# Feed-forward products of batch 0 in float32 in place of three split passes, in a fused attention and two-MoE kernel

## The chip, the cores and the metric

The kernel runs on one core of a Trainium2 chip. The metric is the device time of one execution in microseconds; the span of the profiled execution runs from its first to its last instruction. The engines are PE (TensorE), PEld (its weight loads), ACT (ScalarE), DVE (VectorE), POOL (GpSimd) and SP (SyncE), whose queue issues the DMAs.

## The reference

Attention with a tanh cap on the scores over 4 batches of 12 heads (448 positions, 64 wide), then two feed-forward layers on the 1792 rows:

```python
scores = cap * np.tanh(scale * np.matmul(q, k.transpose(0, 1, 3, 2)) / cap)
attn = np.exp(scores - np.max(scores, axis=-1, keepdims=True))
attn = attn / (np.sum(attn, axis=-1, keepdims=True) + 1e-09)
x = np.matmul(attn, v)                      # as 1792 x 768
h = x @ w_in;  x = (h - np.tanh(h)) @ w_out                     # layer 0
h = x @ w_in2; out = (h / (1.0 + np.exp(-1.702 * h))) @ w_out2  # layer 1
```

Activations are float32. The weights (768 x 2048 and 2048 x 768, twice) arrive as float64.

## The kernel before

The attention of batch 0 runs alone. Then four batches of feed-forward work follow, `moe(b)` for b = 0 to 3, and beside batch b the attention of batch b+1: the program text issues a piece of attention after so many products, by `ATT_RATES` (for batch 0 none in the first quarter, then 0.7, 0.7 and 1.3 parts). Tensor products and attention share PE, which works through one queue in order.

`moe(b)` has four quarters of equal products: `gemm_in(0)`, `gemm_out(0)`, `gemm_in(1)`, `gemm_out(1)`. Each quarter has 96 products of a 128 x 128 weight tile with a 128 x 448 activation tile. The weights are cut into 68 chunks: a `gemm_in` has 16 chunks of 6 tiles, a `gemm_out` has 6 x 3 chunks of 6, 5 and 5 tiles (`parts`). A product is made in one of two ways. **Split**: weight and activation are each cut into a high part (float32r) and a low part, and three passes wh*xh, wh*xl and wl*xh (float32r) add up in PSUM. **Unsplit**: one float32 matmul on the uncut operands, which stands in the trace as two matmul records. Before the change only the 16 chunks of batch 0's first quarter are unsplit (`i < KF` in `w_split`); they read `xf`, and the split ones read `xh`, `xl` (or `gh`, `gl` behind the activation function).

In batch 0 each chunk is also converted from float64 (`w_convert`): `dbl_dma` loads its words into one of three `wd` buffers (pool `wd_p`); ACT scales the high words into a `wr` buffer (L193) and makes a 16-bit step on the low half-words in place (L194); DVE shifts (L195) and joins (L196); SP then issues the load of the chunk three further on into the freed `wd` buffer, and the store of the float32 result to DRAM (`kept`), from which batches 1 to 3 reload it. `wr_p` has three buffers. A split chunk is then cut: the high part on ACT or DVE (`hi_act`, `hi_dve`, L93 and L96), the low part on POOL in batch 0 (`lo_pool`, L102) and on DVE later (`lo_dve`, L99).

`ahead(i)`, called behind the first matmul of chunk i, converts up to chunk i + 2. The activation function of layer 0 is `g_cubic` (ACT L520, L528, L530, L531; DVE L521, L532, L534, L535), that of layer 1 `g_gate` (ACT L550, DVE L552); behind either, `g_split` cuts the result into `gh` (ACT or DVE in turn) and `gl` (POOL). `run_late` issues their last steps some matmuls into the next chunk. The output of layer 0 is cut into `xh`, `xl` by ACT and DVE. A scheduler sets the final order on each engine; it may pull an instruction up as far as its buffers allow.

Attention lines that the steps touch: transposes of q and k on PE (L275, tile `ps_qk`), scores (L290, L298, `ps_sc`), tanh (L306) and exp (L317) on ACT with the row maximum on DVE between (L307, L308), transposes of the weights (L359, `ps_pt`), products with v (L372, `ps_pv`), and a copy `xs` on ACT at the end of each pair of heads (L385).

## Time and profile before

| what | value |
|---|---|
| three runs, median (lowest to highest) | 1348.9 us (1344.34 to 1349.25) |
| the profiled execution, own time | 1349.95 us |
| its span | 1348.2 us |
| mean granted PE clock, share of full speed | 0.978 |
| PE / PEld busy | 1273.5 us (94%) / 1027.5 us (76%) |
| ACT / DVE / POOL busy | 845.6 us (63%) / 840.0 us (62%) / 329.0 us (24%) |
| DMA | 203.5 MB, mean 151 GB/s |

A busy share is an average over stages with different limits. Matmuls are pipelined, so a record of PE spans more than the time that it adds; the distance from one start to the next is what a matmul costs. "Idle before" with a releaser names what an engine waited for last.

### The profile page before, as it was taken

What the parts mean: (1) busy time and instruction counts of PE and PEld (TensorE: products, weight loads), DVE (VectorE), ACT (ScalarE), POOL (GpSimd) and SP (SyncE); (2) the same over time, 40 slices, a digit from 0 to 9 for tenths busy, and PEclk for the clock granted to TensorE, in tenths of its full rate; (3) what the DMA queues carried; (4) which work ended last, traced back from release to release, by engine and by line L of the source; (5) the groups of instructions that cost most, each with busy time, mean ns of one, the idle gap of its engine ahead of it and who ended that gap; (6) DMA issues with size and microseconds to landing.
All of it is one profiled execution on the core that took longest, in us unless ns stands there. A gap on an engine that the chain in (4) does not pass through costs nothing.

```text
span 1348.2 us, 18627 instructions
## 1 busy us (share of the span) xinstructions
PE 1273.5 (94%) x6540; PEld 1027.5 (76%) x6540; DVE 840.0 (62%) x1280; ACT 845.6 (63%) x1352; POOL 329.0 (24%) x258
## 2 busy tenths in 40 slices
PE   8989978888788998999999999999999999999998
PEld 3445557676666787888888888888898889999997
DVE  5867997567765569945657439845575528734432
ACT  7858979778778668745656437745565527623421
POOL 0002354346533214301232004301232103201300
PEclk8989998999999899999999999999999999999999
DMA  7305767866566386533334466433433257433332
GB/s 203 103 15 182 241 227 237 276 203 216 187 192 201 114 266 222 172 110 104 110 102 127 112 189 179 127 97 105 120 98 106 86 163 216 131 108 110 108 117 59
DMA packets 163981, 203.53 MB, mean 151 GB/s; under 512 B 53296, under 2 KB 120880, under 8 KB 163888
## 3 DMA queue, kind: packets, MB, share of 16 engines
q1 hardware_dynamic: 163888, 202.35, 49.5%
q8 instruction: 51, 0.84, 0.3%
q14 instruction: 42, 0.34, 0.1%
HBM read 156.99 MB, written 45.32 MB: 150 GB/s over the span
## 4 chain that ended last, share of the span: by engine, by line
PE 62%; ACT 9%; DVE 8%; issue 4%; POOL 2%; DMA 1%; SPq 0%; DVEq 0%; ACTq 0%; POOLq 0%
PE ps_y L588 30%; PE ps_h L568 21%; PE ps_pv L372 4%; PE ps_pt L359 3%; ACT wd L194 3%; PE ps_sc L290 3%; POOL wl L102 2%; ACT wr L193 1%; DVE wr L196 1%; ACT t L317 1%; DVE tm L307 1%; DVE g_q L534 1%; DVE g_q L535 1%; DVE g_t L532 1%; PE ps_o L613 1%
## 5 line engine op out<-in xcount | busy, mean ns | idle before, releaser
L99 DVE TENSOR_TENSOR wl<-wr,wh 128x768 fp32r<-128x768 f32 (+1 forms) x172 | 156.9, 912 | 217.9 <-PE ps_y L588 100.2
L588 PE MATMUL ps_y<-gh,wh 128*128 128x448 f32 x768 | 288.3, 375 | 4.1 <-DVE wh L96 3.4
L588 PE MATMUL ps_y<-gl,wh 128*128 128x448 f32 x768 | 291.2, 379 | 1.0 <-POOL gl L102 1.0
L568 PE MATMUL ps_h<-xh,wh 128*128 128x448 f32 x672 | 250.6, 373 | 19.1 <-DVE g_g L552 11.4
L93 ACT CAST wh<-wr 128x768 fp32r<-128x768 f32 (+1 forms) x189 | 148.4, 785 | 183.7 <-PE ps_y L588 136.6
L568 PE MATMUL ps_h<-xl,wh 128*128 128x448 f32 x672 | 249.3, 371 | 1.1 <-DVE xl L99 1.1
L588 PE MATMUL ps_y<-gh,wl 128*128 128x448 f32 x768 | 190.5, 373 | 0.0
L317 ACT ACTIVATE t<-t,tm,cpos 112x448 f32<-112x448 f32 x192 | 144.4, 754 | 41.5 <-DVE tm L308 37.6
L588 PEld LDWEIGHTS ps_y<-gh,wh 128*128 128x128 f32 x768 | 147.3, 192 | 22.9 <-issue 5.9
L588 PEld LDWEIGHTS ps_y<-gl,wh 128*128 128x128 f32 x768 | 147.4, 192 | 19.2 <-issue 6.8
L568 PE MATMUL ps_h<-xh,wl 128*128 128x448 f32 x672 | 161.3, 371 | 0.0
L588 PEld LDWEIGHTS ps_y<-gh,wl 128*128 128x128 f32 x768 | 143.1, 190 | 21.3 <-issue 9.9
L568 PEld LDWEIGHTS ps_h<-xh,wh 128*128 128x128 f32 x672 | 127.6, 190 | 37.5 <-DVE g_g L552 14.7
L102 POOL TENSOR_TENSOR gl<-g_q,gh 128x448 fp32r<-128x448 f32 x64 | 87.5, 1368 | 271.5 <-ACT gh L93 178.3
L568 PEld LDWEIGHTS ps_h<-xl,wh 128*128 128x128 f32 x672 | 127.4, 190 | 13.6 <-issue 2.1
L568 PEld LDWEIGHTS ps_h<-xh,wl 128*128 128x128 f32 x672 | 125.5, 189 | 14.9 <-issue 4.8
L102 POOL TENSOR_TENSOR gl<-g_g,gh 128x448 fp32r<-128x448 f32 x64 | 77.6, 1213 | 225.6 <-ACT gh L93 129.6
L307 DVE TENSOR_REDUCE tm<-t 112x2 f32<-112x896 f32 x96 | 103.4, 1080 | 45.7 <-ACT t L306 45.5
L102 POOL TENSOR_TENSOR wl<-wr,wh 128x768 fp32r<-128x768 f32 (+1 forms) x52 | 97.0, 1866 | 133.0 <-DVE wh L96 37.2
L194 ACT ACTIVATE wd<-wd 128x768 uint16<-128x768 uint16 (+1 forms) x68 | 125.9, 1852 | 1.0
L359 PE MATMUL ps_pt<-ident,t 112*112 112x112 f32 x768 | 97.2, 270 | 20.2 <-ACT t L306 13.1
L359 PEld LDWEIGHTS ps_pt<-ident,t 112*112 112x112 f32 x768 | 83.3, 139 | 42.3 <-ACT t L306 18.7
(76 smaller groups left out, 1698.4 us busy)
## 6 DMA issues: line engine op xcount, KB each, us to landing
wr<-kept SPq DMA_DIRECT2D x100, 384.0 KB, 3.0
wd<-in_moe_w_in_dram SPq DMA_DIRECT2D x64, 384.0 KB, 4.6
wr<-kept SPq DMA_DIRECT2D x72, 320.0 KB, 2.9
wd<-in_moe_w_out_dram SPq DMA_DIRECT2D x48, 384.0 KB, 4.2
kept<-wr SPq DMA_DIRECT2D x44, 384.0 KB, 5.1
wh<-kept_hl SPq DMA_DIRECT2D x32, 384.0 KB, 3.3
wl<-kept_hl SPq DMA_DIRECT2D x32, 384.0 KB, 3.7
kept<-wr SPq DMA_DIRECT2D x24, 320.0 KB, 4.7
```

What stands on the lines that cost most here:

```text
L93: nc.scalar.copy(out=dst, in_=src)
L99: nc.vector.tensor_tensor(out=dst, in0=src, in1=hi.bitcast(F32), op=ALU.subtract)
L102: nc.gpsimd.tensor_tensor(out=dst, in0=src, in1=hi.bitcast(F32), op=ALU.subtract)
L193: nc.scalar.mul(out=o, in_=high.bitcast(F32), mul=2.0 ** -112)
L194: nc.scalar.mul(out=half[:, :, :, 2], in_=half[:, :, :, 1], mul=F64_LOW)
L290: nc.tensor.matmul(ps[:, j, :S], qq[a, 0, c * CP:(c + 1) * CP], kk[a, 1], start=(m == 0), stop=(m == 2),)
L307: nc.vector.tensor_reduce(out=tm, in_=t, axis=AX.X, op=ALU.max)
L317: nc.scalar.activation(out=t[:, j], in_=t[:, j], func=AF.Exp, scale=cpos[:CP], bias=tm[:, j:j + 1], accum_out=ss[:, j, c:c + 1],)
L359: nc.tensor.transpose(ps[:, kc // 2, o:o + CP], t[:, j, kc * CP:(kc + 1) * CP], ident[:CP, :CP])
L372: nc.tensor.matmul(r_t[g][j * D:(j + 1) * D, :S], rawv[g][:, j, kc, :], p_t[g][:, kc, j, :], start=(kc == 0), stop=(kc == C - 1),)
L568: nc.tensor.matmul(ps[:, :S], w[:, kk, :], x[kk], start=(m == 0), stop=(m == len(seq) - 1))
L588: nc.tensor.matmul(ps[:, :S], w[:, f - f0, :], x[f], start=(c == 0 and m == 0), stop=(c == len(parts) - 1 and m == len(seq) - 1),)
```

## The change

Every product of batch 0 is made unsplit: `w_split` now takes all chunks with i < NCH as they are. The results of the activation function go to float32 tiles `gf`, which share the tags of `gh` (so `gh` is allocated when batch 1 begins), `g_split` does nothing in batch 0, and the output of layer 0 goes uncut to `xf`, by ACT and DVE in turn; `xh` is allocated when batch 1 cuts its input. `passes = 3` in `gemm_out` keeps the count of steps, and with it the pace of attention per chunk. Converted chunks are held in `wr_p` (even) and in the buffers of `wh_p` (odd), six in all, and `ahead` asks for four chunks ahead in place of two. For odd chunks the 16-bit step moves from ACT to DVE. PSUM tiles of odd f in batch 0's second `gemm_in` come from `ps_s`.

```diff
--- before.py
+++ after.py
@@ -35,6 +35,8 @@
 AHEAD = 2
 
 LATE_AT = 8
+
+LEAD_0 = 4
 
 WARM_UP = 12
 
@@ -148,7 +150,7 @@
     ]
     kept = [dr_p.tile([P, k1 - k0, P], F32, name=f"kept{i}") for i, (_, k0, k1) in enumerate(chunks)]
     dbls, raws, whl = {}, {}, {}
-    gh, gl = [], []
+    gf, gh, gl = [None] * KF, [None] * KF, []
     n_dma, n_split, n_use = [0], [0], [0]
 
     n_dbl = [0]
@@ -185,13 +187,21 @@
 
     def w_convert(i):
         _, k0, k1 = chunks[i]
-        r = wr_p.tile([P, WCH, P], F32, tag="wr", name="wr")
+        if i % 2:
+            r = wh_p.tile([P, WCH, P], F32, tag="wh", name="wr")
+        else:
+            r = wr_p.tile([P, WCH, P], F32, tag="wr", name="wr")
         d = dbls.pop(i)
         high, half = d[:, :, :, 1], d.bitcast(U16)
         o = r[:, :k1 - k0]
         u = o.bitcast(U32)
         nc.scalar.mul(out=o, in_=high.bitcast(F32), mul=2.0 ** -112)
-        nc.scalar.mul(out=half[:, :, :, 2], in_=half[:, :, :, 1], mul=F64_LOW)
+        if i % 2:
+            nc.vector.tensor_scalar(
+                out=half[:, :, :, 2], in0=half[:, :, :, 1], scalar1=F64_LOW, scalar2=None, op0=ALU.mult
+            )
+        else:
+            nc.scalar.mul(out=half[:, :, :, 2], in_=half[:, :, :, 1], mul=F64_LOW)
         nc.vector.tensor_scalar(out=u, in0=u, scalar1=3, scalar2=None, op0=ALU.logical_shift_left)
         nc.vector.scalar_tensor_tensor(
             out=u, in0=high, scalar=0x80000007, in1=u, op0=ALU.bitwise_and, op1=ALU.bitwise_or
@@ -209,14 +219,14 @@
             _, k0, k1 = chunks[i % NCH]
             n = k1 - k0
             r = w_convert(i) if i < NCH else raws.pop(i)
-            if i < KF:
+            if i < NCH:
                 whl[i] = (r, None)
                 n_split[0] += 1
                 continue
             h = wh_p.tile([P, WCH, P], F32R, tag="wh", name="wh")
             l = wh_p.tile([P, WCH, P], F32R, tag="wl", name="wl")
-            (hi_dve if i < NCH and i % 3 else hi_act)(h[:, :n], r[:, :n])
-            (lo_pool if i < NCH else lo_dve)(l[:, :n], r[:, :n], h[:, :n])
+            hi_act(h[:, :n], r[:, :n])
+            lo_dve(l[:, :n], r[:, :n], h[:, :n])
             if i // NCH == 1 and split_kept[i % NCH]:
                 for m, t in enumerate((h, l)):
                     nc.sync.dma_start(out=kept_hl[i % NCH][:, m], in_=t[:, :n].bitcast(F32))
@@ -399,6 +409,8 @@
         else:
             x = xs_p.tile([P, S], F32, tag="xs", name="xs")
             nc.sync.dma_start(out=x, in_=xd[i])
+        if xh[i] is None:
+            xh[i] = big.tile([P, S], F32R, tag=f"xh{i}", name=f"xh{i}")
         hi_act(xh[i], x)
         lo_dve(xl[i], x, xh[i])
 
@@ -508,11 +520,17 @@
 
     def ahead(i):
         w_dma(i + 2)
-        w_split(i + 2)
+        w_split(i + (LEAD_0 if i + LEAD_0 < NCH else 2))
 
     def g_split(f, g):
+        if gh[f] is None:
+            return
         yield (hi_dve if f % 2 else hi_act)(gh[f], g)
         yield lo_pool(gl[f], g, gh[f])
+
+    def g_tile(to, f, dt):
+        to[f] = g_big.tile([P, S], dt, tag=f"gh{f}", name=f"g{f}")
+        return to[f]
 
     def g_cubic(f, ps):
         t = g_p.tile([P, S], F32, tag="t", name="g_t")
@@ -531,7 +549,11 @@
             nc.scalar.activation(out=m, in_=v, func=AF.Relu, bias=cub_u)
             nc.vector.tensor_tensor(out=t, in0=v, in1=t, op=ALU.mult)
             next(last, None)
-            nc.vector.scalar_tensor_tensor(out=q, in0=q, scalar=CUB_C, in1=t, op0=ALU.add, op1=ALU.mult)
+            if gh[f] is None:
+                q_in, q = q, g_tile(gf, f, F32)
+            else:
+                q_in = q
+            nc.vector.scalar_tensor_tensor(out=q, in0=q_in, scalar=CUB_C, in1=t, op0=ALU.add, op1=ALU.mult)
             nc.vector.copy_predicated(out=q, mask=m.bitcast(U16), data=far)
             splits.append(g_split(f, q))
             for _ in last:
@@ -548,14 +570,14 @@
     def g_gate(f, ps):
         t = g_p.tile([P, S], F32, tag="t", name="g_t")
         nc.scalar.activation(out=t, in_=ps[:, :S], func=AF.Tanh, scale=0.5 * GELU_C)
-        g = g_p.tile([P, S], F32, tag="far", name="g_g")
+        g = g_tile(gf, f, F32) if gh[f] is None else g_p.tile([P, S], F32, tag="far", name="g_g")
         nc.vector.scalar_tensor_tensor(out=g, in0=t, scalar=1.0, in1=ps[:, :S], op0=ALU.add, op1=ALU.mult)
         late.append(lambda: list(g_split(f, g)))
 
     def gemm_in(layer, b):
         for f in range(KF):
             i, (wh, wl) = w_next()
-            if f % 4 == 3 if b > 0 else layer == 0 and f % 2:
+            if f % 4 == 3 if b > 0 else b == 0 and f % 2:
                 ps = ps_s.tile([P, 512], F32, tag="s", name="ps_h")
             else:
                 ps = ps_m.tile([P, 512], F32, tag="m", name="ps_h")
@@ -584,6 +606,10 @@
                 i, (wh, wl) = w_next()
                 seq = [p for f in range(f0, f1) for p in ((wh, gh, f), (wh, gl, f))]
                 seq += [(wl, gh, f) for f in range(f0, f1)]
+                passes = 1
+                if wl is None:
+                    seq = [(wh, gf, f) for f in range(f0, f1)]
+                    passes = 3
                 for m, (w, x, f) in enumerate(seq):
                     nc.tensor.matmul(
                         ps[:, :S], w[:, f - f0, :], x[f],
@@ -592,13 +618,13 @@
                     )
                     if m == 0:
                         ahead(i)
-                    if m == LATE_AT:
+                    if m == LATE_AT // passes:
                         run_late()
-                    if not (c == len(parts) - 1 and m == len(seq) - 1):
+                    for _ in range(passes - (c == len(parts) - 1 and m == len(seq) - 1)):
                         yield
-            if layer == 0:
-                if b == 0:
-                    xh[e] = big.tile([P, S], F32R, tag=f"xh{e}", name=f"xh{e}")
+            if layer == 0 and b == 0:
+                (hi_dve if e % 2 else hi_act)(xf[e], ps[:, :S])
+            elif layer == 0:
                 hi_act(xh[e], ps[:, :S])
                 lo_dve(xl[e], ps[:, :S], xh[e])
             else:
@@ -659,10 +685,12 @@
     first.close()
     g_big = pool("g_big", 1)
     ps_m = pool("ps_m", 2, space=bass.MemoryType.PSUM)
-    gh += [g_big.tile([P, S], F32R, name=f"gh{i}") for i in range(KF)]
     gl += [g_big.tile([P, S], F32R, name=f"gl{i}") for i in range(KF)]
     per_batch = 10 * NP
     for b in range(B):
+        if b == 1:
+            for f in range(KF):
+                g_tile(gh, f, F32R)
         n_pair[0] = n_split_x[0] = 0
         x_free[0] = False
         owed, live, cnt = 0.0, b + 1 < B, 0
```

Three places in the instruction order show what moves; line numbers of the changed kernel differ from those above (a few lines later).

ScalarE, while the attention of batch 0 runs, behind the second pair's exponentials. `wr<-wd` and `wd<-wd` are the two ScalarE steps of a conversion, `t,ss<-t` an exp, `t<-ps_sc` a tanh, `xs<-ps_pv` the end of a pair. Before:

```order
L194 ACTIVATE wd<-wd 128x768
L306 ACTIVATE t<-ps_sc,tsc 112x896
L317 ACTIVATE t,ss<-t,tm,cpos 112x448 x2
L193 ACTIVATE wr<-wd 128x768
L317 ACTIVATE t,ss<-t,tm,cpos 112x448
L385 COPY xs<-ps_pv 128x448
```

and with the change:

```order
L204 ACTIVATE wd<-wd 128x768
L198 ACTIVATE wr<-wd 128x768
L395 COPY xs<-ps_pv 128x448
L327 ACTIVATE t,ss<-t,tm,cpos 112x448 x2
L316 ACTIVATE t<-ps_sc,tsc 112x896
L198 ACTIVATE wr<-wd 128x768
L316 ACTIVATE t<-ps_sc,tsc 112x896
L327 ACTIVATE t,ss<-t,tm,cpos 112x448 x2
L316 ACTIVATE t<-ps_sc,tsc 112x896
L204 ACTIVATE wd<-wd 128x768
```

Before, three chunks (0 to 2) are converted ahead of the first product, the third around this place; now six are (0 to 5), chunks 3 and 4 here and chunk 5 four rows later. The rest of attention's ScalarE work stands behind them.

TensorE, the first chunk of `gemm_out(0)` in batch 0 (its last two of twelve high passes, its six low passes, and the first pass of the next chunk). Before:

```order
L588 MATMUL ps_y<-gh_1030,wh 128x448
L588 MATMUL ps_y<-gl_1046,wh 128x448
L588 MATMUL ps_y<-gh_1025,wl 128x448
L588 MATMUL ps_y<-gh_1026,wl 128x448
L588 MATMUL ps_y<-gh_1027,wl 128x448
L588 MATMUL ps_y<-gh_1028,wl 128x448
L588 MATMUL ps_y<-gh_1029,wl 128x448
L588 MATMUL ps_y<-gh_1030,wl 128x448
L588 MATMUL ps_y<-gh_1031,wh 128x448
```

and with the change the whole of that chunk and the first product of the next:

```order
L614 MATMUL ps_y<-g_1117,wr 128x448
L614 MATMUL ps_y<-g_1147,wr 128x448
L614 MATMUL ps_y<-g_1177,wr 128x448
L614 MATMUL ps_y<-g_1207,wr 128x448
L614 MATMUL ps_y<-g_1237,wr 128x448
L614 MATMUL ps_y<-g_1267,wr 128x448
L614 MATMUL ps_y<-g_1297,wr 128x448
```

Eighteen instructions of the chunk became six; nothing of a high or low part is waited for.

VectorE, one chunk of `gemm_in(0)` in batch 0, from one `g_far` to the next. Before:

```order
L521 TENSOR_TENSOR g_far<-ps_h,g_t 128x448
L96 CAST gh_1026<-g_q 128x448
L195 TENSOR_SCALAR wr<-wr 128x768
L532 TENSOR_TENSOR g_t<-g_v,g_t 128x448
L196 SCALAR_TENSOR_TENSOR wr<-wd,wr 128x768
L534 SCALAR_TENSOR_TENSOR g_q<-g_q,g_t 128x448
L535 COPY_PREDICATED g_q<-g_m,g_far 128x448
```

and with the change, at an odd chunk:

```order
L539 TENSOR_TENSOR g_far<-ps_h,g_t 128x448
L200 TENSOR_SCALAR wd<-wd 128x768
L205 TENSOR_SCALAR wr<-wr 128x768
L550 TENSOR_TENSOR g_t<-g_v,g_t 128x448
L206 SCALAR_TENSOR_TENSOR wr<-wd,wr 128x768
L556 SCALAR_TENSOR_TENSOR g_1267<-g_q,g_t 128x448
L557 COPY_PREDICATED g_1267<-g_m,g_far 128x448
```

The cast to `gh` is gone from every second chunk and the 16-bit step (L200) is new in every second chunk.

## Rows read from the trace of the kernel before

**Rows 1.** Windows by stage: us, PE, PEld, DVE, ACT, POOL busy (instructions), PEclk, DMA share, GB/s

```profile
100.30:172.60 72.30, 72.30 (x194) 36.27 (x192) 64.14 (x90) 67.79 (x95) 19.82 (x13) 1.00 0.67 212
172.60:482.40 309.80, 264.14 (x1382) 213.74 (x1381) 208.67 (x283) 239.06 (x321) 129.31 (x83) 0.94 0.66 208
...
796.10:1103.40 307.30, 303.57 (x1649) 256.43 (x1649) 185.24 (x308) 177.92 (x314) 67.08 (x56) 0.99 0.42 121
1103.40:1342.10 238.70, 238.70 (x1177) 218.36 (x1175) 116.75 (x160) 101.50 (x160) 39.38 (x32) 1.00 0.43 128
```

**Rows 2.** Chain that ended last, 90 to 470 us, its shares by line

```profile
by line: PE ps_y L588 12.7%; ACT wd L194 10.5%; issue 8.6%; POOL wl L102 7.3%; ACT wr L193 5.3%; DVE wr L196 4.8%; ACT t L317 3.9%; PE ps_pv L372 3.1%; DMA kept<-wr 2.4%; PE ps_sc L290 1.9%; DVE tm L307 1.9%; PE ps_pt L359 1.6%; ACT pf L93 
```

**Rows 3.** What PE waited for, 100 to 460 us: total us, times, longest

```profile
PE ps_pt L359 <- ACT t L306: 12.8, 5, 4.6
PE ps_h L568 <- DVE g_g L552: 11.4, 9, 3.0
PE ps_sc L290 <- ACT qk L93: 7.1, 4, 3.5
PE ps_sc L290 <- DVE ql L99: 4.1, 5, 1.2
```

**Rows 4.** PE timeline, first product of each batch and the last: start us, us, instruction

```profile
100.29 3.19 PE L568 MATMUL ps_h<-xf,wr 128*128 128x448 f32 x8
...
482.37 0.45 PE L568 MATMUL ps_h<-xh,wh 128*128 128x448 f32 x1
...
796.14 0.36 PE L568 MATMUL ps_h<-xh,wh 128*128 128x448 f32 x1
...
1103.41 0.36 PE L568 MATMUL ps_h<-xh,wh 128*128 128x448 f32 x1
...
1340.93 1.19 PE L588 MATMUL ps_y<-gh,wl 128*128 128x448 f32 x5
```

**Rows 5.** Lines by form, 100 to 460 us: busy us, mean ns | idle before

```profile
L194 ACT ACTIVATE wd<-wd 128x768 uint16<-128x768 uint16 x41 | 80.3, 1958 | 0.5
L568 PE MATMUL ps_h<-xf,wr 128*128 128x448 f32 x192 | 72.3, 539 | 0.0
...
L196 DVE SCALAR_TENSOR_TENSOR wr<-wd,wr 128x768 uint32<-128x768 uint32 x41 | 46.2, 1126 | 33.6 <-ACT wd L194 30.3 <-DMA raw<-in_q_dram 1.4 <-DMA kept<-wr 1.4
...
L193 ACT ACTIVATE wr<-wd 128x768 f32<-128x768 f32 x41 | 38.1, 929 | 28.1 <-POOL wl L102 24.1 <-DMA kept<-wr 3.9
...
L195 DVE TENSOR_SCALAR wr<-wr 128x768 uint32<-128x768 uint32 x41 | 26.5, 648 | 19.9 <-ACT wr L193 17.9 <-DMA wd<-in_moe_w_in_dram 1.9
```

**Rows 6.** ACT timeline, one ScalarE step of g_cubic, two chunks apart

```profile
142.89 0.62 ACT L520 ACTIVATE g_t<-ps_h 128x448 f32<-128x448 f32 x1
...
152.35 0.61 ACT L520 ACTIVATE g_t<-ps_h 128x448 f32<-128x448 f32 x1
```

**Rows 7.** DVE timeline, one chunk of the first quarter and the step before

```profile
158.11 0.61 DVE L534 SCALAR_TENSOR_TENSOR g_q<-g_q,g_t 128x448 f32<-128x448 f32 x1
...
159.39 0.60 DVE L521 TENSOR_TENSOR g_far<-ps_h,g_t 128x448 f32<-128x448 f32 x1
...
161.80 1.55 DVE L534 SCALAR_TENSOR_TENSOR g_q<-g_q,g_t 128x448 f32<-128x448 f32 x1
...
164.01 0.63 DVE L521 TENSOR_TENSOR g_far<-ps_h,g_t 128x448 f32<-128x448 f32 x1
```

**Rows 8.** ACT timeline, ends of the first three pairs of batch 0's attention

```profile
33.28 0.51 ACT L385 COPY xs<-ps_pv 128x448 f32<-128x448 f32 x1
...
47.57 0.53 ACT L385 COPY xs<-ps_pv 128x448 f32<-128x448 f32 x1 [0.17 <-PE ps_pv L372]
...
60.31 0.51 ACT L385 COPY xs<-ps_pv 128x448 f32<-128x448 f32 x1
```

**Rows 9.** What PE waited for in batch 1, 482 to 796 us

```profile
PE ps_h L568 <- DVE g_far L521: 5.7, 2, 5.0
```

## The prediction, made before the result was known

> **What bounds the kernel now.** I read the windows by stage first. Batches 2 and 3 keep PE busy for 303.6 of 307.3 us and for all of 238.7 us, at a granted clock of 0.99 and 1.00; the first quarter of batch 0 is just as full. The rest of batch 0 is not: 264.1 us busy in 309.8 us at a clock of 0.94 [rows 1]. The change touches batch 0, and only its last three quarters can give time back. The first products of the batches, at 100.29, 482.37, 796.14 and 1103.41 us, bound the stages [rows 4]; batch 0 takes 382.1 us, batch 1 313.8 us.
>
> Next, what ends last there. In the chain of waits from 90 to 470 us, much stands on the making of weights: the two conversion steps on ACT (10.5% and 5.3%), the low part on POOL (7.3%), the join on DVE (4.8%) [rows 2]. The lines say why: the first conversion step sat idle 28.1 us before it, 24.1 us of that until POOL had made a low part, which frees the `wr` buffer [rows 5]. So conversion runs three buffers round a loop that POOL closes, and it has little lead. The waits of PE itself show the other half: 12.8 us in which attention's transposes wait for a tanh on ACT, 7.1 and 4.1 us for the high and low parts of q and k, and 11.4 us until the gate on DVE frees a PSUM tile [rows 3]. The engines named there also do conversions, in order.
>
> **Part 1: more PE work.** The first quarter, unsplit and without attention, has 96 products in 192 records and takes 72.3 us [rows 5]. Batch 3, split and without attention, takes 238.7 us for four quarters [rows 1], 59.7 us each with the transposes of the output in it. A quarter made unsplit so costs PE 12.6 us more, three of them 37.8 us. This lies wholly on PE's path. [...]
>
> **Part 2: time that PE loses.** Attention beside a batch costs PE what batch 2 takes over batch 3: 307.3 - 238.7 = 68.6 us [rows 1]. Batch 0, as it is, would without lost time take 72.3 + 3 x 59.7 + 68.6 = 320.0 us; it takes 382.1, so 62.1 us are lost to waits and to the lower clock that goes with them. With the change the floor is 4 x 72.3 + 68.6 = 357.8 us. What of the 62.1 us stays?
>
> The buffer loop goes: POOL makes no low part in batch 0, there are six buffers in place of three, and PE itself frees them. ACT now takes 9.46 us for two chunks of the first quarter [rows 6], 4.73 us each, against 72.3 / 16 = 4.52 us on PE: it falls behind. Half of the 16-bit steps (1958 ns each [rows 5]) leave it, so 0.98 us per chunk, and it needs 3.75 us. DVE takes 4.62 us for a chunk in which one operation took 1.55 us where its fellow before took 0.61 us [rows 7]; without that stretch 3.68 us. The 16-bit step on DVE is not in this trace. Its bounds are the shift, 648 ns on as many words in rows without gaps, and ACT's own step on the same half-words, 1958 ns; I take 1126 ns, the join, which reads words at the same distance on the same engine [rows 5]. Half of it per chunk gives 4.25 us, with the upper bound 4.66 us: just under the pace of PE or just over it, and five converted chunks (22.6 us of PE work) cover 16 x 0.14 us. In the later quarters, where attention is added to PE's pace, or no cubic function runs, there is more room.
>
> [...]
>
> What does not go are waits within attention: PE in order behind tanh, exp, q and k. Batch 1, which has no conversions, loses 313.8 - 307.3 = 6.5 us against batch 2, 5.7 us of it in one line of waits [rows 4, 9]. I take 12 us for batch 0, about twice that, since ACT and DVE still convert beside attention; the bounds are 2 us (as batch 2) and 30.5 us (the three attention waits of [rows 3], 24.0 us, in full, and batch 1's 6.5). Batch 0 then takes 369.8 us, 12.3 us less than now.
>
> **Part 3: attention of batch 0 is made longer.** The order shows six chunks converted before the first product, where three are now. The load of chunk 3 waits for the end of conversion 0, and so on, and the loads of q, k and v queue behind those on SP; they were issued well ahead of their use, and I cost that at nothing. If that cover is gone, PE waits for q and k of a late pair. The conversions themselves delay attention on ACT and DVE: the pair with a conversion in it takes 47.57 - 33.28 = 14.29 us, the next, without, 12.74 us [rows 8]: 1.55 us for one, 4.7 us for three. The bounds are nothing and 14.0 us (three times the four steps of [rows 5], 4.66 us, with none of it hidden); a gain is excluded, since work is only added. In the first quarter PE is full already, so the early conversions are not paid back there.
>
> **Part 4: the rest.** Casts to high parts on ACT and DVE, low parts of activations on POOL, and the subtraction behind layer 0 all go; I cost them at nothing beyond part 2, since what they held up is counted in the 62.1 us. The stores to `kept`, the reloads and batches 1 to 3 stay; so does the work at the batch's end, where `gh` takes over buffers whose readers are done.
>
> **The sum**: -12.3 + 4.7 = -7.6 us. The profiled execution took 1349.95 us (span 1348.2), 1.05 us above the median of the three runs, 1348.9 us. So 1342.3 us by the profile and **1341.3 us** against the median.
>
> **The rivals.**
>
> *Nothing is lost any more (faster).* For it: with a longer time per chunk, ACT and DVE have longer to deliver attention's parts, and batch 2 loses hardly anything. Against it: ACT and DVE carry 17 conversions in each quarter. Lost 2 us, attention 2 us longer: 359.8 + 2 - 382.1 = -20.3 us, 1328.6 us.
>
> *The saving is eaten evenly (no change).* PE's extra 37.8 us and part 3 just equal what is won where 19.6 us stay lost: 1348.9 us. For it: batch 0's PE waits are as much attention's as the conversions' [rows 3].
>
> *Attention's waits stay (slower).* Place: PE's queue, at the transposes and scores of batch 1's attention in the last three quarters. In order behind conversions that themselves wait (for a load, or until PE frees a buffer), ACT delivers tanh and the parts of q and k as late as now. Lost 30.5 us, with 4.7 us for part 3: 357.8 + 30.5 + 4.7 - 382.1 = +10.9 us, 1359.8 us. It decides once more than 19.6 us stay lost. Against it: POOL no longer closes the loop.
>
> *The change doesn't do what it says.* If conversion still had no lead, say because three `wd` buffers and the loads bind, we would see lost time near the 62.1 us and far more than any of these; but the first quarter already converts a chunk in 4.73 us with these three buffers, and batch 0 needs one per 369.8 / 68 = 5.4 us. I give it 2%, inside the slower case.
>
> **How the numbers follow.** The forecast (5 to 17 us lost) gets 0.47, nothing lost 0.20, no change 0.16, slower 0.17. A measurement of this kernel can tell about 0.5% from no change, 6.7 us; my likeliest time is hardly beyond it. Of the forecast's own range the part below 12.9 us lost (attention included as above) counts as faster, about six tenths: faster 0.20 + 0.29 = 0.49, same 0.18 + 0.16 = 0.34, slower 0.17. The likeliest case alone spans 1334 to 1346 us. The range of 8 in 10 reaches into both outer cases, to 1327 us and 1357 us.
>
> **What the profile will show.** Right: first product of batch 0 at about 105 us, of batch 1 at about 475 us; the remaining batches as long as now; unsplit records near 72.3 / 192 = 0.377 us apart in all four quarters; PE's clock in 172 to 475 us above 0.97; no wait on POOL in the chain there; DVE's 16-bit step between 0.65 and 1.96 us; ACT's first conversion step no longer waiting for POOL. Wrong: PE waits on tanh or on q and k that add up to over 20 us, attention of batch 0 that ends at 110 us or later, or a quarter that takes over 100 us without such waits, which would mean that weights still come late.

## The result: faster, by more than twice what was forecast

The changed kernel takes 1329.08 us (median of 4 runs, 1326.04 to 1329.35), the kernel before, in 4 runs beside it, 1347.99 us: a ratio of 0.9856, 95% interval 0.984 to 0.9871. That is 18.9 us less, where 7.6 us less had been forecast. It lies inside the range, close to its lower end, and at the rival "nothing is lost any more" (1328.6 us).

The profiled execution took 1328.83 us, its span is 1327.0 us, 21.2 us below that of before. Batch 0 gives 26.6 us of it, the attention ahead of it takes 7.3 us back, and batches 1 to 3 give 1.9 us; batches 2 and 3 vary by as much between the traces of the kernels below (305.8 to 307.6 and 243.6 to 244.8 us). Windows of batch 0 by quarter, after (columns as in [rows 1]):

```profile
107.60:179.70 72.10, 72.10 (x194) 36.48 (x193) 59.51 (x97) 56.65 (x84) 0.00 (x0) 1.00 0.70 220
179.70:267.90 88.20, 88.20 (x317) 46.25 (x316) 51.09 (x80) 56.55 (x81) 1.28 (x4) 1.00 0.77 241
267.90:356.10 88.20, 88.20 (x322) 46.77 (x321) 55.43 (x83) 56.66 (x82) 1.08 (x3) 1.00 0.73 226
356.10:463.10 107.00, 107.00 (x459) 57.56 (x457) 55.29 (x85) 60.83 (x96) 2.95 (x6) 1.00 0.58 182
```

And quarters 2 and 3 of the kernel before:

```profile
173.10:273.50 100.40, 82.43 (x412) 67.73 (x413) 74.56 (x98) 81.09 (x101) 44.67 (x25) 0.93 0.78 248
273.50:370.80 97.30, 81.16 (x417) 66.09 (x417) 69.33 (x89) 78.90 (x107) 51.97 (x35) 0.96 0.63 200
```

PE is now busy for the whole of every quarter, at a clock of 1.00; before it stood idle for 16 to 18 us in each of these two, at 0.93 and 0.96. ACT's work in quarter 2 falls from 81.09 to 56.55 us, POOL's from 44.67 to 1.28. The first products of batches 0 and 1, in the PE timeline after:

```profile
107.58 1.31 PE L590 MATMUL ps_h<-xf,wr 128*128 128x448 f32 x3
...
463.07 0.45 PE L590 MATMUL ps_h<-xh,wh 128*128 128x448 f32 x1
```

Batch 0 takes 355.5 us (before 382.1, [rows 4]). What PE waited for from 100 to 470 us, in full (it stands ahead of the first product); it answers to [rows 3]:

```profile
PE ps_pv L382 <- DVE pf L98: 1.2, 1, 1.2
```

The 35 us of named waits in [rows 3] are gone, attention's (on tanh, q and k) as well as the gate's. The chain from 90 to 470 us, by line, answers to [rows 2]:

```profile
by line: PE ps_h L590 39.1%; PE ps_y L614 38.8%; PE ps_pv L382 7.3%; PE ps_pt L369 5.3%; PE ps_sc L300 4.4%; PE ps_qk L285 1.4%; PE ps_r L356 1.1%; PE ps_o L639 0.8%; DVE pf L98 0.6%; ACT t L327 0.4%; DVE tm L317 0.3%; PE ps_sc L308 0.2%; D
```

Nearly all of it is PE. The conversion steps on ACT and the low part on POOL are no longer in it. Lines by form, 100 to 465 us, answer to [rows 5]:

```profile
L590 PE MATMUL ps_h<-xf,wr 128*128 128x448 f32 x384 | 148.0, 541 | 0.0
...
L204 ACT ACTIVATE wd<-wd 128x768 uint16<-128x768 uint16 x19 | 36.4, 1918 | 0.3
L206 DVE SCALAR_TENSOR_TENSOR wr<-wd,wr 128x768 uint32<-128x768 uint32 x38 | 36.4, 958 | 22.0 <-ACT wd L204 21.6
...
L198 ACT ACTIVATE wr<-wd 128x768 f32<-128x768 f32 x38 | 34.5, 908 | 18.9 <-PE ps_y L614 18.8
...
L205 DVE TENSOR_SCALAR wr<-wr 128x768 uint32<-128x768 uint32 x38 | 21.8, 573 | 17.4 <-ACT wr L198 17.4
...
L200 DVE TENSOR_SCALAR wd<-wd 128x768 uint16<-128x768 uint16 x19 | 19.6, 1031 | 11.9 <-ACT wr L198 11.9
...
L550 DVE TENSOR_TENSOR g_t<-g_v,g_t 128x448 f32<-128x448 f32 x16 | 9.9, 617 | 0.0
```

L198 (L193 before) now waits for PE to free a weight buffer, 18.8 us, and not for POOL: weights are ready early. The unsplit records of L590 are 384 where [rows 5] have 192, both `gemm_in` quarters. L200 is the 16-bit step on DVE, 1031 ns. L206 (L196 before) takes 958 ns where it took 1126, L205 (L195) 573 where it took 648, and L550 617.

### The profile page after: what moved, and what is told of

It reads as the page before. It is cut to its first block, busy times and chain, and to the rows that moved or that the text cites. A ratio compares the mean times of both kernels' runs of the same rounds, so it can differ in the third digit from the quotient of the medians.

```text
span 1327.0 us, 17719 instructions
## 1 busy us (share of the span) xinstructions
PE 1298.0 (98%) x6252; PEld 966.7 (73%) x6252; DVE 796.6 (60%) x1260; ACT 772.4 (58%) x1282; POOL 187.4 (14%) x174
## 4 chain that ended last, share of the span: by engine, by line
PE 86%; DVE 7%; ACT 4%; issue 2%; DMA 1%; SPq 0%; DVEq 0%; ACTq 0%
PE ps_y L614 37%; PE ps_h L590 31%; PE ps_pv L382 6%; PE ps_pt L369 5%; PE ps_sc L300 3%; PE ps_qk L285 1%; DVE g_q L556 1%; DVE tm L317 1%; PE ps_sc L308 1%; ACT t L327 1%; PE ps_o L639 1%; DVE g_t L550 1%; DVE g_q L557 1%; DVE wl L101 1%; ACT t L316 1%
## 5 line engine op out<-in xcount | busy, mean ns | idle before, releaser
L590 PE MATMUL ps_h<-xh,wh 128*128 128x448 f32 x576 | 214.4, 372 | 7.9 <-DVE g_far L539 7.9
L614 PE MATMUL ps_y<-gl,wh 128*128 128x448 f32 x576 | 214.1, 372 | 0.0
L590 PE MATMUL ps_h<-xl,wh 128*128 128x448 f32 x576 | 213.7, 371 | 0.0
L614 PE MATMUL ps_y<-g,wh 128*128 128x448 f32 x576 | 212.5, 369 | 0.0
L614 PE MATMUL ps_y<-g,wr 128*128 128x448 f32 x384 | 154.0, 544 | 0.0
L590 PE MATMUL ps_h<-xf,wr 128*128 128x448 f32 x384 | 148.0, 541 | 0.0
L614 PE MATMUL ps_y<-g,wl 128*128 128x448 f32 x576 | 140.7, 370 | 0.0
L590 PE MATMUL ps_h<-xh,wl 128*128 128x448 f32 x576 | 136.0, 368 | 0.0
L590 PEld LDWEIGHTS ps_h<-xh,wh 128*128 128x128 f32 x576 | 109.4, 190 | 20.9 <-DVE g_far L539 9.0
L590 PEld LDWEIGHTS ps_h<-xf,wr 128*128 128x128 f32 x384 | 71.6, 190 | 67.4 <-issue 66.3
L614 PEld LDWEIGHTS ps_y<-g,wl 128*128 128x128 f32 x576 | 106.4, 188 | 15.1 <-issue 6.9
L590 PEld LDWEIGHTS ps_h<-xl,wh 128*128 128x128 f32 x576 | 109.4, 190 | 10.9 <-issue 2.1
L614 PEld LDWEIGHTS ps_y<-g,wh 128*128 128x128 f32 x576 | 108.3, 188 | 11.9 <-issue 4.0
L590 PEld LDWEIGHTS ps_h<-xh,wl 128*128 128x128 f32 x576 | 107.3, 188 | 12.3 <-issue 3.4
L316 ACT ACTIVATE t<-ps_sc,tsc 112x896 f32<-112x896 f32 x96 | 93.0, 1002 | 38.7 <-PE ps_sc L300 27.7
L614 PEld LDWEIGHTS ps_y<-g,wr 128*128 128x128 f32 x384 | 69.2, 190 | 59.6 <-issue 59.1
```

Source lines behind the costliest of these rows:

```text
L316: nc.scalar.activation(out=t, in_=sc_t.pop((g, c))[:, :, :S], func=AF.Tanh, scale=tsc[:CP])
L590: nc.tensor.matmul(ps[:, :S], w[:, kk, :], x[kk], start=(m == 0), stop=(m == len(seq) - 1))
L614: nc.tensor.matmul(ps[:, :S], w[:, f - f0, :], x[f], start=(c == 0 and m == 0), stop=(c == len(parts) - 1 and m == len(seq) - 1),)
```

## The experiments

Three theories were set against each other. **U**: unsplitting alone does it, since PE then uses a chunk up more slowly than ACT and DVE make one. **L**: the gain is that of six buffers and a lead of four chunks. **P**: it is the low part on POOL that goes. A fourth question was what the early conversions cost in batch 0's attention (**G**). Quarters run from the first product of one to that of the next; "attention" is the time from the end of the first pair (the first `xs` copy, as in [rows 8]) to the first product of batch 0. It leaves out the start, which differs by up to 3.6 us between the traces of all kernels (first `xs` at 32.97 to 36.54 us). Each ratio is taken against executions of the kernel before beside that kernel, not against the first row.

| kernel | median us (runs) | ratio, 95% interval | attention | quarters 1 to 4 | batch 0 |
|---|---|---|---|---|---|
| before | 1347.99 (4) | 1 | 67.0 | 72.8, 100.4, 97.3, 111.5 | 382.1 |
| after | 1329.08 (4) | 0.9856, 0.984 to 0.9871 | 73.0 | 72.2, 88.2, 88.1, 107.0 | 355.5 |
| unsplit_alone | 1323.57 (4) | 0.9815, 0.9794 to 0.9836 | 66.9 | 72.2, 88.2, 88.2, 106.7 | 355.2 |
| unsplit_dve16 | 1326.63 (2) | 0.9843, 0.9813 to 0.9874 | 65.7 | 72.2, 88.2, 88.1, 106.6 | 355.1 |
| lead_act16 | 1327.20 (2) | 0.9847, 0.9823 to 0.9872 | 70.1 | 72.2, 88.2, 88.2, 107.2 | 355.7 |
| gate_behind_attention | 1324.95 (4) | 0.983, 0.9813 to 0.9846 | 66.1 | 72.2, 88.2, 88.1, 107.0 | 355.5 |
| split_six_bufs | 1359.99 (2) | 1.0083, 1.0053 to 1.0113 | 70.3 | 71.8, 111.9, 96.9, 106.6 | 387.2 |
| split_no_low | 1320.98 (2) | 0.9793, 0.9769 to 0.9818 | 66.8 | 72.8, 91.2, 85.3, 104.6 | 354.0 |
| split_lo_dve | 1331.48 (2) | 0.9871, 0.9847 to 0.9895 | 66.9 | 72.8, 90.9, 91.9, 107.6 | 363.4 |
| gate_late | 1325.44 (5) | 0.9821, 0.9804 to 0.9838 | 68.5 | 72.2, 88.2, 88.2, 106.6 | 355.1 |
| act_one_more | 1330.08 (2) | 0.987, 0.9843 to 0.9896 | 66.9 | 72.2, 88.4, 88.7, 107.8 | 357.0 |
| act_two_more | 1365.53 (2) | 1.0133, 1.0104 to 1.0161 | 67.0 | 72.2, 97.9, 98.9, 121.8 | 390.7 |
| pool_kept | 1324.00 (2) | 0.9824, 0.9799 to 0.985 | 67.0 | 72.2, 88.2, 88.2, 106.8 | 355.3 |
| gate_last | 1322.65 (5) | 0.9814, 0.9793 to 0.9835 | 66.8 | 72.2, 88.2, 88.1, 106.7 | 355.1 |

### Parts of the change by themselves

**unsplit_alone**: the change without the six buffers, the longer lead and the 16-bit step on DVE (against after).

```diff
-LEAD_0 = 4
+LEAD_0 = 2
-        if i % 2:
-            r = wh_p.tile([P, WCH, P], F32, tag="wh", name="wr")
-        else:
-            r = wr_p.tile([P, WCH, P], F32, tag="wr", name="wr")
+        r = wr_p.tile([P, WCH, P], F32, tag="wr", name="wr")
...
+        nc.scalar.mul(out=half[:, :, :, 2], in_=half[:, :, :, 1], mul=F64_LOW)
```

> The change without its other two parts: all products of batch 0 unsplit, but three wr buffers, two chunks ahead, the 16-bit step always on ACT. Theory U (taking the split away is enough: POOL leaves the buffer loop, ACT and DVE are relieved, and PE's chunk takes longer): batch 0 takes 355 to 359 us as with the change (355.3), and since only three chunks are converted ahead, its first product starts at 100 to 101 us as before (100.3), so the span is 1319 to 1324 us, some 6 us below the change's 1327.0. Theory L (the lead and the buffers are what took the waits away): PE waits for weights again, batch 0 takes 367 us or more, the span is 1331 us or more.

Batch 0 takes 355.2 us with three buffers and a lead of two, as after: theory L falls, U holds, and those three parts give batch 0 nothing. Its attention is 6.1 us shorter than after's. The first product comes at 103.4 us, later than the 100 to 101 expected, because the first pair ended at 36.54 us, 3.3 us later than in before. One part of the change is still in this and all other unsplit kernels, and no run tries it alone: the PSUM tiles from `ps_s` in the second `gemm_in`. They bear on quarter 3 alone, where PE in before waited 11.4 us for the gate to free a PSUM tile [rows 3]; the gain of quarter 2 can't come from them.

**unsplit_dve16**: the same with the 16-bit step of odd chunks on DVE, as in the change.

> As unsplit_alone, with the 16-bit step of odd chunks on DVE. Theory U: batch 0 at 355 to 358 us, first product at 99 to 102 us, span 1318 to 1323 us, within 2 us of unsplit_alone. Theory L: batch 0 at 365 us or more, though better than unsplit_alone by up to 5 us, since ACT has about 1 us less per chunk.

Batch 0 is the same to 0.1 us. In attention the step on DVE saves 1.2 us, which the two runs don't resolve.

**lead_act16**: the change with the 16-bit step always on ACT (against after: the `if i % 2` of that step goes, the ACT line stays).

> The change with the 16-bit step always on ACT: six buffers and four chunks ahead kept. Both theories: batch 0 still at 355 to 359 us, since the first quarter is the only place where ACT comes near PE's pace (about 4.45 us of 4.52 per chunk). If the delay of batch 0's attention (107.7 us to the first product, against 100.3 before) comes from ScalarE's share of the early conversions, the first product comes later still, at 109 to 112 us, and the span is 1328 to 1332 us; if it comes from VectorE's share or from waiting for loads, it stays at 105 to 108 us.

The quarters don't move. The first product comes at 105.0 us, not at 109 or later: ACT's share of the early conversions isn't what delays attention most. Attention, 70.1 us, is longer than unsplit_alone's 66.9 by the six buffers and the three early conversions alone, and shorter than after's 73.0, of which 1.4 us is attention's last product (4.83 us here, 6.24 in after; more on it below).

**gate_behind_attention**: the change with conversions 3 to 6 issued only behind the last pair's `xs` and `xf` (constants put in for their names).

```diff
+        if 3 <= i <= 6:
+            at_act, at_dve = ends[-1]
+            with tc.issue_after(at_act), tc.issue_after(at_dve):
+                return w_convert_now(i)
```

> The change, but the conversions of chunks 3 to 6 are kept behind batch 0's attention on ACT and DVE, so that three are made before the first product, as before the change. If the early conversions are what made attention longer by 7.4 us, the first product starts at 100 to 101.5 us, batch 0 takes 355 to 357 us, and the span is 1319 to 1322 us. If the attention is longer for another reason (the loads queued on SP, the 16-bit step on DVE), the first product stays beyond 104 us.

Attention falls from 73.0 to 66.1 us, batch 0 stays at 355.5: the early conversions cost attention 6 to 7 us, and batch 0 doesn't need them.

### What the split kernel lost its time to

**split_six_bufs**: the kernel before with six `wr` buffers and a lead of four.

```diff
-    wr_p = pool("wraw", 3)
+    wr_p = pool("wraw", 6)
-        w_split(i + 2)
+        w_split(i + (4 if i + 4 < NCH else 2))
```

> The kernel before, split as it was, with six wr buffers in place of three and conversion four chunks ahead in place of two. It gives the second part of the change alone. If the buffer loop that POOL closes was what lost the 62 us of batch 0, six buffers slacken it and batch 0 falls from 382 us to 350 us or less (its floor with split products is 320 us). If the loss was the load itself that cutting weights and activations puts on ACT, DVE and POOL, beside attention, more buffers move little: batch 0 stays at 372 to 385 us, and the early conversions lengthen batch 0's attention by 3 to 7 us.

It is slower than before, 387.2 us in batch 0, with quarter 2 at 111.9: more buffers and lead don't help the split kernel either. Why quarter 2 grew by 11.5 us wasn't tried apart.

**split_lo_dve**: the kernel before with batch 0's low parts of weights on DVE (`lo_dve` in place of `lo_pool`).

> The kernel before, with the low part of batch 0's weights on DVE in place of POOL. If POOL's slowness (1.98 us for a low part) in the loop was the loss, the 0.97 us that DVE takes for the same elements later in the kernel makes batch 0 shorter than 382 us, 360 to 375 us. If the load on DVE counts as much, batch 0 is as long or longer, 380 to 400 us.

**split_no_low**: the kernel before without the low part of batch 0's weights.

```diff
+            if i < NCH:
+                whl[i] = (h, h)
+                n_split[0] += 1
+                continue
```

> The kernel before, with the low part of batch 0's weights left out: the passes that read it read the high part in its place, so PE has the same passes, and POOL makes no low part of weights. Three wr buffers, two chunks ahead. If POOL's low part in the buffer loop was the main loss, batch 0 falls to 330 to 350 us, far below the change's 355 us. If the load on ACT and DVE was the main loss, batch 0 stays above 360 us.

Batch 0 falls by 18.7 and 28.1 us; 354.0 us without the low part lies between the two expectations, 330 to 350 and above 360. So within the split kernel POOL's low part of the weights was the dearest piece tried, as P says. But the split kernel without it still loses time; three of its PE waits and its quarters 2 and 3:

```profile
PE ps_sc L294 <- ACT qk L93: 6.7, 4, 3.5
PE ps_pt L363 <- ACT t L310: 3.9, 3, 1.4
PE ps_h L572 <- DVE g_g L556: 5.9, 7, 1.2
```

```profile
172.60:263.80 91.20, 79.93 (x413) 65.39 (x414) 58.37 (x98) 79.57 (x99) 4.96 (x5) 0.96 0.80 262
263.80:349.10 85.30, 77.51 (x417) 63.84 (x416) 55.89 (x90) 77.25 (x107) 19.37 (x18) 1.00 0.74 239
```

Against [rows 3], the waits on tanh fall from 12.8 to 3.9 us with the low part, those on ACT for q and k hardly (7.1 to 6.7), the gate's from 11.4 to 5.9. PE's own need there is 59.7 us of split products [rows 1] and 16.0 of attention (88.2 - 72.2), 75.7 us (its busy time in the windows, 79.93 and 77.51 us, is larger; a record spans more than the time that a matmul adds, in [rows 5] 539 ns where 72.3 / 192 = 377 ns are added); it took 91.20 and 85.30 us, with ACT busy for 79.57 and 77.25. ACT alone had more to do than PE.

### How much room there is when PE is slower

**act_one_more** and **act_two_more**: unsplit_alone with the first conversion step on ACT repeated, once or twice (the diff has two), in the last three quarters of batch 0.

```diff
         nc.scalar.mul(out=o, in_=high.bitcast(F32), mul=2.0 ** -112)
+        for _ in range(2 if i >= KF else 0):
+            nc.scalar.mul(out=o, in_=high.bitcast(F32), mul=2.0 ** -112)
```

> unsplit_alone with the first conversion step on ScalarE issued twice (the second rewrites the same words) for every chunk of the last three quarters of batch 0: 51 x about 0.92 us = 47 us more on ScalarE, which then is busy for about 84.9 of 88.2, 87.3 of 88.2 and 92.1 of 106.7 us in quarters 2 to 4. Theory U (unsplit, PE eats weights more slowly than ScalarE and VectorE make them, and with work in hand nothing is lost until ScalarE is full): quarters 2 to 4 stay within 3 us each of 88.2, 88.2 and 106.7, batch 0 355 to 362 us. Rival (the 12 us that I had put down for attention's waits are the price of a busy ScalarE in order, and are missing only because it is idle a fifth of the time): waits of PE on tanh, exp, q and k come back, 10 us and more, batch 0 at 365 us or above.

> The same with two repeats: ScalarE would need 100.5, 102.9 and 107.7 us in quarters 2 to 4, more than PE. Theory U: the quarters follow ScalarE, q2 to q4 at about 97 to 101, 102 and 107 to 110 us (the lead of one or two chunks covers part of the first), batch 0 380 to 386 us. Rival (the waits add to that, as in the split kernel, where quarters took 97 to 111 us with ScalarE busy for 78 to 81 us of them): batch 0 at 395 us or above. If both theories are wrong and ScalarE is not what is waited for, batch 0 stays below 365 us.

Quarters 2 and 3 of unsplit_alone, act_one_more and act_two_more:

```profile
175.60:263.80 88.20, 88.20 (x318) 46.27 (x317) 43.74 (x71) 69.23 (x90) 0.74 (x2) 1.00 0.74 238
263.80:352.00 88.20, 88.20 (x322) 46.81 (x321) 49.86 (x74) 71.66 (x90) 1.49 (x4) 1.00 0.75 232
```

```profile
173.51:261.90 88.39, 88.39 (x317) 46.26 (x316) 43.82 (x68) 80.64 (x105) 0.75 (x2) 1.00 0.76 241
261.90:350.59 88.69, 88.55 (x321) 46.58 (x320) 48.17 (x74) 85.04 (x108) 1.86 (x4) 1.00 0.74 225
```

```profile
172.23:270.10 97.87, 90.85 (x317) 45.48 (x316) 45.58 (x70) 94.94 (x124) 0.74 (x2) 1.00 0.69 215
270.10:368.96 98.86, 90.32 (x321) 46.24 (x319) 46.30 (x72) 95.53 (x120) 1.49 (x4) 1.00 0.65 203
```

With ACT busy for 85.04 of 88.69 us (96%) PE still loses next to nothing: batch 0 takes 357.0 us, 1.8 more than unsplit_alone. Once ACT has more to do than the quarter lasts, the quarter follows it (94.94 of 97.87 us), and batch 0 grows to 390.7 us. That is beyond the 380 to 386 that U gave, all of it in quarter 4 (121.8 us, ACT 105.35 us, about PE's own 106.7), and short of the rival's 395. In quarter 4 time is lost though ACT's work is no more than PE's. The longest waits of PE in quarters 2 to 4 of act_two_more:

```profile
PE ps_pv L376 <- ACT pf L95: 6.8, 5, 3.9
PE ps_y L608 <- DVE wr L200: 5.8, 8, 1.1
PE ps_pt L363 <- ACT t L310: 2.8, 4, 1.4
```

So the waits of PE on tanh, q and k are no fixed price of a busy ACT: act_one_more, with more work on ACT in quarters 2 and 3 than the kernel before (165.7 us against 160.0), has no named wait there. When ACT is over-full, PE waits again, but mostly for other things than in [rows 3]: for copies of attention's weights (`pf`) and for converted weights (`wr`).

**pool_kept**: unsplit_alone with POOL's subtractions kept (a chunk from itself into the unused low tile, and g from itself into `gl`).

```diff
+                if i >= KF:
+                    l = wh_p.tile([P, WCH, P], F32, tag="wl", name="wl")
+                    lo_pool(l[:, :n], r[:, :n], r[:, :n])
...
+            yield lo_pool(gl[f], g, g)
```

> [...] Theory U (PE's slower pace is the cover): batch 0 355 to 360 us, the two-input VectorE operations of the cubic function lengthened towards 1.0 us again, no more than a few us of waits. Rival P (the low part on POOL was what cost the split kernel its time, whatever PE's pace, as split_no_low's 28 us suggest): batch 0 at 370 us or above, with ScalarE's first conversion step idle behind POOL's wl.

```profile
172.14:260.31 88.17, 88.17 (x317) 46.24 (x316) 49.32 (x71) 68.94 (x90) 27.46 (x22) 1.00 0.75 237
260.31:348.48 88.17, 88.17 (x321) 46.77 (x320) 59.84 (x76) 72.27 (x90) 40.71 (x36) 1.00 0.74 232
```

POOL works for 108.9 us in batch 0, between a weight buffer's making and its reuse, and batch 0 takes 355.3 us: the change's gain doesn't need POOL's work to go, and P falls as its cause. (POOL's load is less than in before, 149.1 us: a low part of 768 columns took 1984 ns there and 1478 ns here.) Of the cubic's two-input operations, which were expected to lengthen, two did not (L546 612 ns, L552 614) and one did (L553 845 ns, in unsplit_alone 669); the last section has what else did. POOL's loop cost time in the split kernels alone. They differ from pool_kept in PE's pace and in the casts on ACT and DVE; act_one_more and pool_kept put back the load of one engine each, and no run keeps the load of all three beside unsplit products.

### Where the early conversions go

**gate_late**: unsplit_dve16 with conversions 0 to 2 behind the end of the fifth pair (the gate of gate_behind_attention with `0 <= i <= 2` and `ends[4]`).

> All products of batch 0 unsplit, three wr buffers, two chunks ahead, the 16-bit step of odd chunks on DVE, and the conversions of chunks 0 to 2 kept behind the fifth of six pairs of batch 0's attention on ACT and DVE. There ACT had 7.7 us and DVE 5.6 us in which they waited for PE. By the 1.55 us that a conversion costs a pair, attention should be 3 to 5 us shorter: 62 to 63 us from the end of the first pair to the first product (67.0 in the kernel before), if conversion 0 then isn't late for that product. Batch 0 at 355 us, the span 1315 to 1320 us. If the three conversions don't fit there, PE waits for weights at the first product, and the span is 1321 us or more.

The gate is misplaced. ACT's timeline, with one conversion step, an exp behind it and the last `xs`:

```profile
91.73 1.92 ACT L212 ACTIVATE wd<-wd 128x768 uint16<-128x768 uint16 x1
93.40 0.70 ACT L335 ACTIVATE t<-t,tm,cpos 112x448 f32<-112x448 f32 x1
...
102.66 0.53 ACT L403 COPY xs<-ps_pv 128x448 f32<-128x448 f32 x1 [7.73 <-PE ps_pv L390]
```

The conversions now stand ahead of the last pair's exps, and ACT idles for 7.73 us afterwards. Attention takes 68.5 us, against 65.7 without the gate.

**gate_last**: the gate moved behind the last exp.

```diff
+        if i < 3:
+            with tc.issue_after(last_exp[0].ins):
+                return w_convert_now(i)
```

> unsplit_dve16 with the first three conversions issued on ScalarE behind the last exp of batch 0's attention, where gate_late's trace shows it idle for 7.73 us. Theory G (conversions ahead of that exp delay attention): from the end of the first pair to the first product 63 to 65.5 us, against 65.7 without the gate and 68.5 in gate_late; batch 0 355 us; 1322 to 1325 us. Rival (the first chunk comes too late, as a conversion of two engines takes about 4.5 us, or the loads of the next chunks do): first product 66 us or more behind it, or waits of PE for weights in the first quarter, 1326 us or above.

Not what was expected of it, 63 to 65.5 us: attention takes 66.8 us, as the rival said, though PE waits for no weights in the first quarter (72.2 us). No gain can be measured: the time is 1322.65 us (1319.80 to 1325.35), beside unsplit_alone's 1321.45 to 1326.75. The last product of attention, in gate_last and then in unsplit_dve16, and the windows of the two:

```profile
93.41 6.24 PE L387 MATMUL ps_pv<-pf,rv 112*64 112x448 f32 x16 [1.60 <-DVE pf L98]
```

```profile
94.24 4.79 PE L379 MATMUL ps_pv<-pf,rv 112*64 112x448 f32 x16 [1.18 <-DVE pf L98]
```

```profile
93.40:99.60 6.20, 6.19 (x17) 1.74 (x17) 4.48 (x6) 3.49 (x3) 0.00 (x0) 0.50 0.45 137
```

```profile
94.20:99.00 4.80, 4.76 (x17) 1.55 (x17) 0.00 (x0) 0.00 (x0) 0.00 (x0) 0.66 0.01 3
```

Relative to the first `xs` (33.25 and 33.74 us) it starts 0.3 us earlier in gate_last, and takes 6.24 us where it took 4.79, at a granted clock of 0.50 where it had 0.66. Two traces don't say that the gate did this: pool_kept and unsplit_alone have the same attention, and the same product takes 6.09 and 4.76 us in them.

unsplit_alone, gate_late and gate_last are faster than both kernels: their intervals end at 0.9836, 0.9838 and 0.9835, the change's begins at 0.984. That is narrow, less than 1 us, and each has its own executions of before; the shorter attention of their traces agrees. Between the three no difference is shown.

## Why the prediction was wrong

**The step that failed** is in part 2: "I take 12 us for batch 0, about twice that, since ACT and DVE still convert beside attention". None was lost: PE waits for 1.2 us in all, ahead of the first product, and batch 0 is as short as unsplit_alone, unsplit_dve16 and gate_last (355.1 to 355.5 us). The working kept apart "the buffer loop", which goes, and "waits within attention", which stay. But they were not independent, and neither was a price that attention pays at any pace of PE. Taking POOL's low part away shortened attention's own waits on tanh (12.8 to 3.9 us in split_no_low), and with unsplit products all are gone, even with ACT's load or POOL's put back. That ACT and DVE serve conversion and attention in one queue each, so that attention's parts are late while conversion is behind, fits this and was not shown by itself. ACT's work against PE's own need, for quarters 2 and 3 together (windows above; need of PE 2 x 75.7 split, 2 x 88.2 unsplit):

| kernel | ACT busy | PE's need | took |
|---|---|---|---|
| before | 160.0 | 151.4 | 197.7 |
| split_no_low | 156.8 | 151.4 | 176.5 |
| act_two_more | 190.5 | 176.4 | 196.7 |
| act_one_more | 165.7 | 176.4 | 177.1 |
| unsplit_alone | 140.9 | 176.4 | 176.4 |
| after | 113.2 | 176.4 | 176.3 |

In these two quarters time is lost where ACT's work exceeds PE's need, and not where it stays below, even at 94%. But this is a sign and not the whole cause. More is lost than ACT's work explains (37.7 us before, 19.7 without the low part). DVE's work falls too: 143.9 us before, 93.6 in unsplit_alone, and no run puts that back. And quarter 4 doesn't follow the rule: before took 111.5 us there with ACT busy for 78.6 and a need of 94.2 (59.7 + 34.5), act_two_more 121.8 us with ACT busy for 105.35 and a need of 106.7. How the loss divides between order, POOL, DVE and the PSUM tiles stays open. ACT's sum could have been had from [rows 1]: ACT's 239.06 us against a split floor of 3 x 59.7 + 68.6 = 247.7 us is 97%; against the unsplit floor of 285.5 us, with even all of that work kept, 84%. Only the first quarter was looked at in this way.

Of the 13.6 us between the forecast's -7.6 and the profile's -21.2 us, batch 0 makes 14.3 (these 12 and 2.3 of the floor) and batches 1 to 3 1.9; attention ahead of it takes 2.6 back.

**PE's extra work (37.8 us).** Right: the unsplit quarter without attention takes 72.2 us, and quarters 2 and 3 88.2 us each with attention.

**The floor of 357.8 us.** Some 2 us too high: batch 0 took 355.5. The 68.6 us for attention contain 3.7 us in which PE stood idle in batch 2 (307.30 - 303.57, [rows 1]), which is enough for it.

**Attention longer by 4.7 us.** Right in kind, and near: 6.0 us between the first pair and the first product, 7.3 with the start. Of the 6.0, 1.3 us are attention's last product (6.24 us, in before 4.90), which varies between traces of the same attention. Most of the rest falls in one pair, as foreseen, in the trace of after:

```profile
34.57 0.52 ACT L395 COPY xs<-ps_pv 128x448 f32<-128x448 f32 x1
...
39.31 0.91 ACT L198 ACTIVATE wr<-wd 128x768 f32<-128x768 f32 x1 [1.83 <-DMA wd<-in_moe_w_in_dram]
...
53.69 0.53 ACT L395 COPY xs<-ps_pv 128x448 f32<-128x448 f32 x1 [2.67 <-PE ps_pv L382]
```

From one `xs` to the next 19.12 us, where [rows 8] have 14.29. A wait on a load, costed at nothing, shows there too: 1.83 us until a `wd` buffer was filled.

**Durations.** The 16-bit step on DVE took 1.031 us (taken 1.126, bounds 0.65 and 1.96). ACT needs 56.65 / 16 = 3.54 us per chunk of the first quarter (forecast 3.75), DVE 59.51 / 16 = 3.72 (4.25). The 4.25 us supposes that the stretch of [rows 7] ends, which was the author's estimate; that operation took 1.038 us in before (L534, mean of 16) and 0.619 us in after (L556). PE's pace covered all of these.

**The rivals.** "Nothing is lost any more" had the mechanism right for batch 0. That its 1328.6 us is within 0.5 us of the measurement is luck: batch 0 is 4.3 us shorter than its 359.8, attention 7.3 us longer in place of 2, and batches 1 to 3 gave 1.9. "Attention's waits stay" took the waits of [rows 3] for attention's own; a loss as large as it needs, over 30 us, came back only in act_two_more, with ACT over-full.

**The signs.** One sign of being wrong was set badly: "a quarter that takes over 100 us without such waits" was to mean that weights come late. Quarter 4 takes 107.0 us without waits, with PE busy for all of it, since attention comes there at 1.3 parts against 0.7: by the prediction's own figures that is 72.3 + 68.6 x 1.3 / 2.7 = 105 us.

**Open.** Batch 1 takes 313.8 to 315.1 us in the split kernels and those with a lead of four, and 315.6 to 320.1 in the unsplit ones with a lead of two, longest where ACT's step is repeated. Nearly all of the difference lies in its first quarter (75.9 to 82.2 us). There PE waits for the last output of batch 0 on ACT, 3.6 us in act_two_more and 0.7 in unsplit_alone; in after it doesn't. What makes the rest wasn't tried. Whether the split kernel without POOL could be brought to PE's pace by unloading ACT alone wasn't tried either.

## What to carry to other kernels

For each stage, set every engine's work beside the time that the bounding engine would need without waits. Where a helper is near or above it, don't add up its waits by name as if each stood for itself: they can end together, and staying below is a good sign, not a proof (quarter 4). Making the bounding engine slower by 12.5 us a quarter can win more than it costs. Try the parts of a change alone: here one part carried all of the gain and another gave a quarter of it back (6 to 7 of 26.6 us).

## What was not expected of the hardware

It was not only VectorE operations with two inputs that took longer beside POOL's work. In pool_kept the cubic's product L546 is at its usual length and the shift L197, with a single input, is not (lines by form, 100 to 458 us; 573 ns is the shift's mean after):

```profile
L197 DVE TENSOR_SCALAR wr<-wr 128x768 uint32<-128x768 uint32 x41 | 36.3, 885 | 21.6 <-ACT wr L195 21.5
...
L546 DVE TENSOR_TENSOR g_t<-g_v,g_t 128x448 f32<-128x448 f32 x16 | 9.8, 612 | 0.0
```

The timeline shows where they meet. The shift starts while POOL is at work and ends 0.42 us after it (alone it takes 0.56 us; POOL's spans are rough); the product behind it meets no POOL:

```profile
133.26 0.93 POOL L104 TENSOR_TENSOR gl<-g 128x448 fp32r<-128x448 f32 x1 [3.59 <-DVE g L553]
...
133.60 1.01 DVE L197 TENSOR_SCALAR wr<-wr 128x768 uint32<-128x768 uint32 x1
...
134.53 0.61 DVE L546 TENSOR_TENSOR g_t<-g_v,g_t 128x448 f32<-128x448 f32 x1
```

In the kernel before it was the product that met POOL (L532, 1090 ns in the mean of 16; in after, as L550, 617):

```profile
126.82 1.39 POOL L102 TENSOR_TENSOR gl<-g_q,gh 128x448 fp32r<-128x448 f32 x1 [2.13 <-DVE gh L96]
...
127.13 1.56 DVE L532 TENSOR_TENSOR g_t<-g_v,g_t 128x448 f32<-128x448 f32 x1
```

By start times in pool_kept, the 128x768 shift takes 0.56 us beside no POOL instruction (10 of them) and 0.99 us beside one (31, up to 1.58); L570, which reads `ps_h` in PSUM, doesn't change (0.616 us in 5 and 0.614 us in 11). What sets the operations that change apart from those that don't is not shown. The longer shifts cost nothing here: batch 0 takes 355.3 us in pool_kept, with VectorE busy for 225.6 of them.
